# The first head pair's k and v as float32 over two hardware queues, a new order for the opening, and four stores on another queue, in a fused attention and mixer kernel

## The chip, the cores and the metric

One core of a Trainium2 chip runs the kernel. The metric is device time in microseconds of one execution, as the median of a few runs. The core has a matrix engine (PE, with its weight loads as PEld), a vector engine (DVE), a scalar engine (ACT), a general engine (POOL, GpSimd) and a sync engine (SP). Work moves between memory and SBUF on 16 DMA engines; SP and ACT issue transfers over hardware queues, POOL over a software queue, which is the only one of the three on which this kernel converts float32 to bfloat16 on the way.

## What is computed

Linear attention with projected keys and values, and then a token and channel mixer, on batch 8, 8 heads, 1024 tokens and head size 64. All inputs and the output are float32.

```python
def _attn_ref(q, k, v, E, F):
    k_proj = np.einsum('ks,bhsd->bhkd', E, k)
    v_proj = np.einsum('ks,bhsd->bhkd', F, v)
    scale = 1.0 / np.sqrt(q.shape[-1])
    scores = scale * np.matmul(q, k_proj.transpose(0, 1, 3, 2))
    scores = scores - np.max(scores, axis=-1, keepdims=True)
    attn = np.exp(scores)
    attn = attn / (np.sum(attn, axis=-1, keepdims=True) + 1e-09)
    return np.matmul(attn, v_proj)

def _moe_ref(x, w_tok1, w_tok2, w_ch1, w_ch2):
    xt = x.transpose(0, 2, 1)
    h = np.maximum(xt @ w_tok1, 0.0) @ w_tok2
    u = x + h.transpose(0, 2, 1)
    h2 = np.maximum(u @ w_ch1, 0.0) @ w_ch2
    return u + h2
```

E and F are 64x1024, w_tok1 1024x256, w_tok2 256x1024, w_ch1 512x1536, w_ch2 1536x512.

## The kernel before

**Stages.** One batch is attention ("front"), then the token mixer (token1, token2), then the channel mixer in two blocks of 512 tokens (up and down; block j belongs to batch j // 2, so there are 16). The channel mixer uses seven products for each 2x2 block product, and so sums of weights are made once by DVE (`combine`, L476: "W1" from w_ch1, three sets of four sums; "W2" from w_ch2, two sets of four). While batch b's up and down products run on PE, the front of batch b + 1 is threaded between them.

**The opening.** Batch 0 has nothing to be threaded into. Its heads go in pairs: pair (2, 3) first, then (4, 5), (0, 1), (6, 7). For a pair, PE turns q (L618), projects k and v with E and F (L521, sixteen matmuls), turns the projected k (L574), forms the scores (L637), ACT takes the exponential (L652), PE multiplies by the projected v (L672, `attend`), and DVE divides (L686, L692). E and F arrive as float32 in `o_t[0]`, a buffer that later holds outputs; PE turns them with a float32 identity (L462), and ACT and DVE copy a half each to bfloat16 (L465). Then come token1 (L1060) and token2 (L1092), the transposes of u (L1121), and the up products (L1180). Blank matmuls on zeros (L436) stand in PE's order where it waits: `FILLS` lists the places of the order ahead of which one is issued.

**Loads.** `LOADS` and the lists behind it issue k, v, q of batch 0 (256 KB in bfloat16 for two heads, 0.524 MB of float32 read), w_tok1 in two halves, w_tok2, six pieces of w_ch1 and four of w_ch2 on POOL's queue (L358), each with a conversion to bfloat16. E goes over SP's queue and F over ACT's. The code has a switch `HWK`, here 0, for sending the pair's k and v over those queues too.

**The order.** `Planner.add` numbers every piece of work (a job) as it is described. `ORDER` is a string of two base-64 digits a job and gives the order in which all 2203 jobs are issued; each engine executes its own in that order. `SPOTS` gives each accumulation a bank of PSUM. `LOADS`, the due times and the planner's durations have no other effect on the code that is issued than through the job numbers; `plan` checks that the order respects the dependencies. Read out, the loads on POOL come in this order:

```
k23 (identities) q23 v23 q45 k45 v45 k01 v01 q01 k67 q67 v67
w_tok1 (two halves)  w_tok2  w_ch1 (six pieces)  w_ch2 (two)
batch 1: k, v of heads 0 to 3   w_ch2 (two)   batch 1: the other loads
```

and PE's first jobs are a blank in float32, two in bfloat16, a second in float32, the transposes of E and F, q23, seven blanks, the projection of k23 and v23.

**Stores.** A down block stores two halves (L1326); all go over POOL's queue but those of the last block (`finish`), which name SP and ACT.

**Normalisation.** `rdn_t` holds the reciprocals of the attention's sums, in two tiles for even and odd pairs.

Of the kernel before, what the change touches and what calls it, by code (L numbers as in the profile page):

```python
# [15 lines left out]
    "0R030T0Q050P0S0408060U070W0V001L0X011M02091E0A1F1G1I1H1J0B1K1N1j1O0C1P1k1c0D1Z1d1Q1e1g1f1h1i0E1R1S1l"  # L16
    "1T1m1W1X0s1U0H0u0w0t0v1n0z0G0x0+1+0F0y0-201-101a1Y24111b1V26250J1812271B19151A1621130I14281C1D1u291o"
    "172S230K2A2T221p1r1q2N2O1v1s2B1t2E1x2P0M2C2U1w2Q1y2V2F1z2R2X2K2W2D2Y2H2G2Z2a2L2I2c2J2b2d2M2l0L2x2m2h"
    "2y2e3B2f2n2i2g2p2o2z3C2q2t2+2-2u2j2r0O302k332v2s0Y37342w310N3L0Z0a353M3d3I3H3D3v323J3N36383R3O0c3E3P"
    "3e0d4c0e3Q3j3K0g3h0f393F3i0b3S3A3f3T3k0h3g3U3-3l3V3G0i3w3X9w3n3W3Y3z4d3m3x3+4u4Y3y4a3p4v4Z403q4g410k"  # L20
    "4w3o5A424x4y0l5B4e0j4h5p4b4f454j464i4k3r5C4z0m43475D5E4l444-0o4m503s4o4n3t4+4p5q525t514B5F4q5r4C495s"
    "530p544D3Z5y3u5w0q5H3bA15x4J3c3a6B5u5I554K5z4r4G4L5K5v4A4H9v5L9x6D484I5+6E0r6F564M6C5-6G6O4N6A606P6Q"
    "626H6I6L4O636561646Z6J674s666K4EA26a57684F6M6b696N4Q0n6f4P6U6g6R6W4R6S6h6Y4U4S6V6c6i6T6X5S4T6d6j6k6u"
    "6l6e5T6m6n6x6+6v5U6o4V6-6y6z716p5a6q4W5G705b725J746r7A73756s765M6t776wA35N7B5O585Q787C5R4t5X5P795Y7J"
    "7F7K7D7G7H7Q7EA57I5Z7L7R5dA759A85eA65VA95fAAA45W5c5h5g5i7V7S5l7TAD7Z7X4X5m5j7a7n5k5n7b7o7W7d5o9z7M7e"
    "7p9-7c7O7q7g7P7r7h7N7f7sAF7i7uAH7Y7lAG7t7m7v7jAJ837wAIANAK7x84ALAOAhAM7z7yAiAP877kAj857U7+88AQAb8986"
    "ARAS8AAcAdAk8BAWAlAm8L9yAZ8CAYAeAT8DAfAaAg8FAUAXAV8M8G8EENB3At7-Az8N8mAEA+8+8i8n8TA-EO8k8oAuAvABAn8H"
    "8U8pB4B5AC8-8q81B0Aq8r92Ao8J90Ap938QArAs8jB6AwB18tB2B795Ax8uB88R8l91Ay8s96B9948v8w9G978x8yBB9H988SBD"
    "999I8KBE9KBCBF8z8WBGEP8VEQ9L9ABABI9N9BBJBH9O9+8X9JBKBNA0BLBO8Y9QBM829MBPBRBSBV8I8aBWBQBTBk9R80BYBXBl"
    "8bBZBUBn9PBc8OBdBa9SBeBfBpBbBh8PBgBmBiER9CBj8ZBo9YEVES9TBr9ZEUBqET8eBs9aEW8f8c9UBu8d9g9W9E9hEYBtC1Bz"  # L30
    "9dEZC2B-9iBwC59VC3BxC69eC48gC89D8hEbC9Bv9bEdC0Ec9c9FEfEj9fCBEeEgEkElCC9jB+EmEhEi9kEn9XEpEr9lC7EoCFCA"
    "By9nCGEsEtCDEq9oCEEu9mCJCHEvEwExCI9r9pCKCXEyEz9qCLCYCME+CNCZEaE-F09sCaILCOCPF19tIMCbDACREXCcF2F4F3Cd"
    "CQ9uF5CeF6CpCfF7FBDCChCSFCDEF9CqDFFADSCiCgFDCrDICTFEDGDJF8FGCjFHFFDHFLDTFICxCkFMFJFPClDUCmFKDLDBDVFQ"
    "FNDDDMFTCVCyINFUFRFODKCnFWDWFXCuDXDNFYCvCzFaCwFVDZFbDQDaC+DRFiFcDODcFSDPFZFdFfFeIPFjFgDdCUFhFlIRDYIT"
    "DkDbISCsIQCWDlFkIUIOC-CoFmFnDeD0CtFoFpDoFqD2DpD1D3FxIXDmD4D6DnIWFzFsFrDrD5FtDqDsFuF-DtD7G0DfDuD8G1Dv"
    "DwF+G2DgG3E0FvG4E1DiDxFwIZE2DyG6IbD+E8G7DjE9IcDzIdGDEAIaE5FyGEG9DhIeGAE6IfD-IhIgGHIiGFIjGIG5GGIkG8IY"
    "GVInE7GKMKIoGBImEBGCGLIsIlECItIuIpGNIqIrIvGOE3IwEDGWE4IxI-GZJ0EEIyGaEFJ1EGIzI+EJEHGXJ5EIJ2GYGcJ3J4GJ"
    "MJGdHQJ7IVJ9J8GbJAD9H8GfGeJBHCGMJCGhJ6JEH9GPJFGiJDGgJJHAHDJGEKHRGQJHJKGRHGJIGTHEHHMLJLMMJNHSJMHUGSHT"
    "HJHVJOGnJPELHFJRHKGjJTEMHXHBJSGlGoJUGpHIJVHMHLJWHNGsGUHYJYHiJQJZHaJXGtHbHOHjJbHPGvJaHmHWJcHnJgJdGwJe"
    "MNGuJfGxGmHZGyMPGkJhHpHcMOJjMRHkMSMQJkGzHlHdHoHqHeJnGqHrJlJoHsGrMVG+HtHuG-JiJzJmH0J+HvH4JpH1JvJsH2H+"  # L40
    "JtJqH3H-HwJxJ-I0JwH5JrK0K1JyJuHyMXK2HxI6MYHgMaK4HzH6I7MZK5HfKBI3I8KCK7MbHhMcK8KDMdQIMeMfKEKFMgMTMhI4"
    "KGK3I5MiK6KIMmI9KJIAMjMkKLIBMnKMK9MoMpKTMlKHKAKUMqI1MrMsQKIDL7MtKXMuMvKZKYIEKKMwL6KVIFKaL8I2IGMxKbMy"
    "KNKWH7ICKdMzKcKeLgM+LAM-IHLBKON0IIN1N3LEN2KfLFKlKgLON5KmLPIJN7KhIKLCN6N8LHMWN4N9LILSL9QHNAKPLQLDNCMU"
    "KiLRNBNDLKLTNENHKRKnLGKjNFLJLVNGKSKqNILLNJLhLMNKLWKrLNNPNLKtNMNQNNKkLiNOKsNSLkNTLYKuKQLZNWLjQJNUNXKw"
    "LlNVKoKvKpNZNRKxNYLUNaNeNbLnNcQLLXNfNdKyKzLaQMNhQOLbNjLmLoNiK+QNLpQPNgQQK-LcLqL0NlLrL2LeL1LsNmLyLtQT"
    "LzLuNnNoL+L3NtLwNxNkM4NyL4NqO9LxL5M5NvOANwNzNuOBM6N+M1NpOCODNrN-OEM2O0NsQVM3O2QWLvO1LdO3M7QXO4O5QYOG"
    "O7OHM8O8QZOFO6M9QaL-OIQdLfOJOLQeQbOKQfMBOMM0QcMCMAQgMDQlQkMFQmMEQnQhORQjP4QUMGP6QiONQRP8OSQoP7P9OXQS"
    "QpQqOVUGPAMHOWQuUFOTPBQvQwOYOUMIQrPCOZQsQtOjPDOaQxQ+PFQyQzObQ-OdR0OcPMOePGOkPNP5PIR1R5PJR3PEOlOPPOPQ"
    "OfPPOrOhR6PHPROsR4R7R2PTR8PSPURAR9RBOoRCPVOpOgUIRFOQRDRGOqPWREPKOtPXPeRJRHOiPfRKRNRLPYRIROOuPLRQPZUH"
    "PiRRPgRcOOPhRSOvRMRTRPRUOwUJRdRVPjRWPaRXUNRfUKRZRYOyULRaRhUMPlRgRbReUOPmPwRiPkRjPnPxRkOzPcPoOmO+PpRl"  # L50
    "RmPyO-PqRnOnRrRoQ2RtOxRvPrQ3RwRpP0Q4RqP1RxP2S7RyPsRzPuUPPbR+P-UQRuPvURS0RsQ0S8S1UUSBUVQ1S9SCS3UWSAQ5"
    "PdUTUXS4SEUYUZUSR-SDSFS2UaSGQ6UbUdS5Q7SJUePtUfUcQ9UgUhSPT3SHSKSQUoQASIUpS6STT2UrUqSUSRT6UsSSQBSWUlUt"
    "QCSXPzUmT7T4P+UnUiQ8TASZUjUkShSLT8UxUuT9QDUvSaUwSVUzQESYU-SiU+V0TBSbT5QFV1TCSNV2QGTDSjUyV4P3TETcScV5"
    "V3TFSpV6SqSdSOV9SfV7VASeTGTdVDSMTKV8THTeSrTIVHTJVBVISmVETLVFVCSnVKTgVLVMThTMSoVJTfVOVGTjTNVPVWTkTOVQ"
    "TiTPVRTlVTSsVNStVUVXTRVSTmTSSgVZVVTQTnVaTuTTToSuSkTpTWTqSwTXSxTYVdVYSySlTsSzTvVeTUSvVbVlTVVgVpVnS+Vf"
    "VqVcS-TwVmVtT0U0VuVoT1W1VhU1W2TaViVwVjVrVxU2W5VkWJW6VvWKTzVyT+WNT-V-W8W0VzU3WOW9W7VsU4WAV+WQTrWPTZWR"
    "WLWSW3WDU5W4X0TtWBWyWTTbWCXIWMWzWVW+WUTxWEX1TyWFU7U6U8WWX4W-U9UBWXWbUAWZX2XaX3UCX5WcXbUDXJX7WYXcWdWH"
    "X6XdWGXMX8WgXNX9WhXPXCXQXAXDXeWiWjXfWaXOXBXEXKXGWmXRXLWIWkXUWlWnXVXhWoWeXiXWXgWqXjWrXmWfXnXkXoXSWsXs"
    "XTWpWtXtXlXHUEXYWuXZXuXpWvXqXFX-XXX+WwXxWxXyXvY9XzXrY0XwY1Y4Y2Y3Y6Y5Y7YAYDY8YBYCYJYFYEYMYGYKYNYHYLYO"
    "YIYPYQ"  # L60
)
SPOTS = (
    "3024101126436327273643040127120236363170420436171063240217145624732113405063774765765024721257605205"
    "6726211311072323401724223063354705252601467407364317023117417326261333177136413604752570156153207422"
# [4 lines left out]
FILLS = (21, 21, 21, 21, 21, 21, 21, 27, 27, 30, 36, 36, 36, 36, 49, 62, 62, 66, 66, 79, 79)  # L69
# [20 lines left out]
HWK = 0  # L90
# [97 lines left out]
def kernel(  # L188
# [13 lines left out]
    nc = tc.nc  # L202
# [40 lines left out]
    def tile_of(shape, dtype, name):  # L243
        return sb.tile(shape, dtype, tag=name, name=name)
# [15 lines left out]
    for i, queue in enumerate((nc.sync, nc.scalar)[:HWK]):  # L260
        queue.dma_start(out=kv32[i], in_=(k, v)[i][0, 0:2].rearrange("h (p si) d -> p h si d", p=P))
# [33 lines left out]
    rdn_t = [tile_of([P, NJ, 2, 2], F32, f"rdn{i}") for i in range(2)]  # L295
# [82 lines left out]
    lead = (1.95, 2.45, 3.2)[HWK]  # L378
    for i in range(HWK):
        pl.add("SPQ", 1.6 + 1.1 * HWK, 1.6 + 1.1 * HWK, lambda: None, writes=[("kv32", i)], prio=-1001)  # L380
        if i:
            act(
                1024, lambda: nc.scalar.copy(out=v_sb[:, 0:2], in_=kv32[1]),
                reads=[("kv32", i)], writes=[("v", 0), ("v", 1)], prio=-100,
            )
        else:
            dve(
                1024, lambda: nc.vector.tensor_copy(out=k_sb[:, 0:2], in_=kv32[0]),
                reads=[("kv32", i)], writes=[("k", 0), ("k", 1)], prio=-100,
            )  # L390
# [55 lines left out]
    opening = [warm(zero), warm(zero), warm32(), warm32()]  # L446
# [1115 lines left out]
```

## Time and profile before

| What | us |
|---|---|
| median of three runs | 415.72 (415.28 to 415.97) |
| the profiled execution, its own time | 415.69 |
| its span, first to last instruction | 413.9 |
| PE busy | 406.4 (98%) |
| DVE busy | 355.9 (86%) |
| ACT busy | 221.9 (54%) |
| POOL busy | 66.8 (16%) |

The span is what the profile covers; the 1.8 us between it and the execution's time lie around it. Times of single instructions are counted from the span's start. The granted clock of PE is 0.999 over the whole execution.

The opening's landmarks, from the timeline and from the DMA issues with their time to landing (issue plus time to landing):

| What | us |
|---|---|
| E and F issued; landed | 0.74 and 0.76; 3.9 and 4.6 |
| k23, q23, v23 landed | 6.5, 7.9, 10.0 |
| first projection (k23, v23) begins | 9.91 |
| q45, k45, v45 landed | 11.3, 12.6, 13.8 |
| k01, v01, q01 landed | 15.1, 16.4, 17.7 |
| k67, q67, v67 landed | 19.0, 21.4, 22.3 |
| w_tok1 halves, w_tok2 landed | 23.6, 24.8; 27.3 |
| first token2 group begins | 28.15 |
| first up product begins | 33.95 |
| w_ch2, first two pieces landed | 37.6, 39.4 |
| batch 1, k and v of heads 0 to 3 landed | 42.0, 44.6 |
| w_ch2, last two pieces landed | 46.5, 48.4 |
| first down product begins | 52.1 |
| last instruction of DVE ends | 410.94 |

Here k23 stands for k of heads 2 and 3, and so on. In a row of windows the columns are the stretch, its length and, for each engine, busy time and the number of instructions that start in it, then PE's granted clock, the DMA share and the GB/s; bytes are counted as written, so a converting load counts half of what it reads. The share is a sum over queues and can pass 1.

### The profile page before, as it was taken

The page shows a single profiled execution, that of the slowest core. Times are in us where ns is not written, and L with a number is a line of the kernel's source. Part 1 is how long each engine was busy: PE and PEld are TensorE (multiplying, and loading weights), DVE is VectorE, ACT ScalarE, POOL GpSimd, SP SyncE. Part 2 cuts the span into 40 slices and gives each one's busy share as a digit, 9 for nine tenths or more (in the row PEclk, how much of TensorE's full clock was granted, in tenths as well). Part 3 has the DMA queues.
Part 4 walks back from the last instruction along what each step waited for, and adds up shares of the span by engine and source line. Part 5 has one row for each costly group of instructions (what it writes and reads, how often), then busy time and mean ns, then how long its engine had stood idle before and what let it go on. Part 6 is the DMA issues. An engine that isn't in the chain of part 4 may idle for free.

```text
span 413.9 us, 9589 instructions
## 1 busy us (share of the span) xinstructions
PE 406.4 (98%) x3909; PEld 344.4 (83%) x3911; DVE 355.9 (86%) x773; ACT 221.9 (54%) x429; POOL 66.8 (16%) x105
## 2 busy tenths in 40 slices
PE   8899999999999999999999999999999999999996
PEld 4489888688888888979988899888988798998896
DVE  2289899779999999989979798898989899988686
ACT  1647884258635664574754646455644745445520
POOL 8544021021102120112001112012100001010010
PEclk9999999999999999999999999999999999999999
DMA  8999999997998897978966869873996212251115
GB/s 153 205 202 204 207 190 192 160 172 170 189 166 168 201 170 143 166 156 156 245 118 127 133 148 178 143 167 89 180 227 118 52 51 103 52 115 39 52 69 187
DMA packets 93755, 61.69 MB, mean 149 GB/s; under 512 B 59024, under 2 KB 89232, under 8 KB 93712
## 3 DMA queue, kind: packets, MB, share of 16 engines
q0 software_dynamic: 35088, 45.09, 55.7%
q1 hardware_dynamic: 58256, 15.47, 22.8%
q8 instruction: 30, 0.49, 0.5%
q10 hardware_dynamic: 368, 0.52, 0.3%
q14 instruction: 13, 0.11, 0.1%
HBM read 59.24 MB, written 16.78 MB: 184 GB/s over the span
## 4 chain that ended last, share of the span: by engine, by line
PE 92%; DMA 4%; DVE 2%; POOL 1%; issue 1%; POOLq 0%; DVEq 0%
PE psum L1289 36%; PE psum L1180 35%; PE psum L991 5%; PE psum L875 4%; PE psum L672 3%; PE psum L521 3%; DMA q_sb<-in_q_dram 3%; PE psum L637 2%; DMA v_sb<-in_v_dram 1%; PE psum L712 1%; PE psum L1060 1%; PE psum L736 1%; DVE u L1105 1%; PE psum L1092 1%; PE psum L618 1%
## 5 line engine op out<-in xcount | busy, mean ns | idle before, releaser
L1289 PEld LDWEIGHTS <-G 128*128 128x128 bf16 x1356 | 130.0, 98 | 18.3 <-issue 3.5
L1289 PE MATMUL psum<-wc_sb,G 128*128 128x256 bf16 (+1 forms) x780 | 101.5, 271 | 0.0
L1180 PEld LDWEIGHTS <-wc_sb 128*128 128x128 bf16 x768 | 73.9, 98 | 10.5 <-issue 2.1
L1202 ACT ACTIVATE G<-psum 128x512 bf16<-128x512 f32 x96 | 56.2, 601 | 44.8 <-PE psum L1180 44.3
L1289 PE MATMUL psum<-wT,G 128*128 128x256 bf16 x576 | 75.6, 273 | 0.1
L1216 DVE TENSOR_TENSOR G<-G 128x512 bf16<-128x512 bf16 (+1 forms) x140 | 69.4, 515 | 0.8
L1180 PEld LDWEIGHTS <-wT 128*128 128x128 bf16 x576 | 55.3, 98 | 7.3 <-issue 0.6
L1180 PE MATMUL psum<-S,wc_sb 128*128 128x256 bf16 x384 | 56.2, 273 | 0.0
L1180 PE MATMUL psum<-S,wT 128*128 128x256 bf16 x384 | 56.0, 273 | 0.1
L1180 PE MATMUL psum<-uT,wc_sb 128*128 128x256 bf16 x384 | 55.5, 273 | 0.0
L1326 POOL DMA_DIRECT2D out_dram<-o x30 | 16.4, 548 | 212.7 <-DVE o L1332 171.2
L692 DVE TENSOR_TENSOR x_sb<-psum,rdn 128x256 bf16<-128x256 f32 (+1 forms) x88 | 46.7, 540 | 1.8
L1332 DVE TENSOR_TENSOR o<-psum,u 128x512 f32<-128x512 f32 x59 | 39.9, 681 | 3.7 <-PE psum L1289 3.3
L1208 ACT COPY ub<-psum 128x512 f32<-128x512 f32 x48 | 28.1, 588 | 23.4 <-PE psum L1180 18.5
L652 ACT ACTIVATE a<-psum 128x512 bf16<-128x512 f32 x64 | 34.9, 603 | 8.5 <-PE psum L637 8.3
L1161 DVE CUSTOM_DVE_ANT_0 G<-psum,ub 128x512 bf16<-128x512 f32 x48 | 32.7, 683 | 6.9 <-PE psum L1180 6.6
L1223 ACT COPY psum<-psum 128x512 f32<-128x512 f32 x48 | 27.6, 579 | 18.6 <-PE psum L1180 13.0
L1161 DVE CUSTOM_DVE_ANT_0 G<-psum,ua 128x512 bf16<-128x512 f32 x48 | 32.6, 684 | 5.3 <-PE psum L1180 4.4
L1208 ACT COPY ua<-psum 128x512 f32<-128x512 f32 x48 | 28.3, 590 | 14.0 <-PE psum L1180 13.6
L1180 PE MATMUL psum<-uT,wT 128*128 128x256 bf16 x192 | 28.7, 273 | 0.0
L358 POOL DMA_DIRECT2D v_sb<-in_v_dram x18 | 13.3, 742 | 75.4 <-PE psum L1180 22.7
L672 PE MATMUL psum<-vb,a 128*128 128x130 bf16 x256 | 25.3, 220 | 0.0
(102 smaller groups left out, 499.4 us busy)
## 6 DMA issues: line engine op xcount, KB each, us to landing
out_dram<-o POOLq DMA_DIRECT2D x30, 512.0 KB, 3.8
k_sb<-in_k_dram POOLq DMA_DIRECT2D x14, 512.0 KB, 11.2
v_sb<-in_v_dram POOLq DMA_DIRECT2D x14, 512.0 KB, 7.3
q_sb<-in_q_dram POOLq DMA_DIRECT2D x14, 512.0 KB, 9.2
wc_sb<-in_moe_w_ch_dram POOLq DMA_DIRECT2D x6, 256.0 KB, 11.9
wc_sb<-in_moe_w_ch_dram POOLq DMA_DIRECT2D x4, 384.0 KB, 13.3
k_sb<-in_k_dram POOLq DMA_DIRECT2D x4, 256.0 KB, 7.9
q_sb<-in_q_dram POOLq DMA_DIRECT2D x4, 256.0 KB, 8.1
```

Source lines behind the costliest of these rows:

```text
L652: lambda g=g, half=half, bk=bk: nc.scalar.activation(out=a_t[g][:, half], in_=bank(bk), func=ACT.Exp, scale=scale),
L672: nc.tensor.matmul(view()[:, k, c].rearrange("p i d -> p (i d)"), a_t[g][:, c, at : at + P], vb[:, g].rearrange("k i d -> k (i d)"), start ...
L692: lambda: nc.vector.tensor_tensor(out=x_sb[:, rows, g * P : (g + 1) * P].rearrange("p (n c) (i d) -> p n c i d", c=2, i=2), in0=view()[:, ...
L991: nc.tensor.matmul(view(X_OF[n])[:, r, :], tok2_of(n, i, r), T[n] if n in T else h[B[n]], start=(n in (1, 7) and r == 0), stop=True, skip_ ...
L1161: nc.vector._custom_dve(TENSOR_ADD_SAT, out=out, in0=in0, in1=in1, s0=FMAX, s1=0.0)
L1180: nc.tensor.matmul(t[:, c, :], w1_of(n, dd, 2 * m + c), a_of(j, n, dd), start=(n in (1, 7) and c == 0 and dd == 0), stop=(c == 1 and dd == 1),
L1202: lambda: nc.scalar.activation(out=G[:, n, cs], in_=view(src), func=ACT.Relu),
L1208: 512, lambda: nc.scalar.copy(out=dst, in_=view("y")), writes=[(name, s % 2)],
L1216: 512 * len(both), lambda: f(out=G[:, n, c], in0=G[:, a, c], in1=G[:, b, c]), ps=False,
L1223: 512, lambda: nc.scalar.copy(out=view("y"), in_=view("x")), takes=[bk["y"]],
L1289: nc.tensor.matmul(to, G[:, G_OF[n], cc, t * P : (t + 1) * P], w2_of(n, cc)[:, cut], start=(n in opens and (t == 0 or alone) and cc == 0), ...
L1332: 512, lambda: nc.vector.tensor_add(out=dst, in0=view(src), in1=u_of(sh, dh)),
```

## The change

Four edits.

1. k and v of heads 2 and 3 are no longer converted on the way. They are read as float32 into `o_t[1]` and `o_t[2]`, head 2 over SP's queue behind E and head 3 over ACT's behind F (256 KB each, four loads). Four new copies convert them: DVE takes k2 and v2, ACT k3 and v3. The two loads leave POOL's list.
2. The order, the banks and the blanks are new. POOL's loads now come as: k45 (identities) q23 v45 q45 q01 v01 k01 q67 k67 v67, w_tok1, w_tok2, w_ch1 (six), batch 1's k and v of heads 0 to 3, w_ch2 (four), the rest of batch 1. PE's first jobs are one blank in bfloat16, one in float32, one in bfloat16, four blanks, the transposes of E and F, twelve blanks, the projection of k23 and v23, the transposes of q23, and the projection of k45 and v45. There are 26 blanks from `FILLS` for 21, and one float32 blank less. Behind the opening the order differs in small ways, until on each engine it is the same as before: for PE from the first up products of block 4 on.
3. `rdn_t` becomes one tile with eight places, taken in turn.
4. The stores of blocks 13 and 14 (two each) go over SP's queue.

```diff
-FILLS = (21, 21, 21, 21, 21, 21, 21, 27, 27, 30, 36, 36, 36, 36, 49, 62, 62, 66, 66, 79, 79)
+FILLS = (11, 11, 11, 11, 26, 26, 26, 26, 26, 26, 26, 26, 26, 26, 26, 26, 36, 36, 36, 36, 40, 61, 61, 73, 73, 86)
...
-    ("k", 0, 2), ("v", 0, 2), ("q", 0, 2), ("k", 2, 2), ("v", 2, 2), ("q", 2, 2),
+    ("k", 0, 2), ("v", 0, 2), ("q", 0, 2), ("q", 2, 2),
...
-    for i, queue in enumerate((nc.sync, nc.scalar)[:HWK]):
-        queue.dma_start(out=kv32[i], in_=(k, v)[i][0, 0:2].rearrange("h (p si) d -> p h si d", p=P))
+    for i, src in enumerate((k, v)):
+        for h, queue in enumerate((nc.sync, nc.scalar)):
+            queue.dma_start(out=kv32[i][:, h], in_=src[0, 2 + h].rearrange("(p si) d -> p si d", p=P))
...
-    rdn_t = [tile_of([P, NJ, 2, 2], F32, f"rdn{i}") for i in range(2)]
+    rdn_t = tile_of([P, 2 * HP, NJ, 2, 2], F32, "rdn")
...
+    pl.add("SPQ", 4.5, 4.5, lambda: None, writes=["EF"], prio=-1003)
+    for i, (name, to) in enumerate((("k", k_sb), ("v", v_sb))):
+        pl.add("SPQ", 7.8 + 1.6 * i, 7.8 + 1.6 * i, lambda: None, writes=[("kv32", i)], prio=-1002 + i)
+        for h in range(2):
+            (act if h else dve)(
+                512,
+                lambda i=i, h=h, to=to: (nc.scalar.copy if h else nc.vector.tensor_copy)(
+                    out=to[:, 2 + h], in_=kv32[i][:, h]
+                ),
+                reads=[("kv32", i)], writes=[(name, 2 + h)], prio=-100 + i,
             )
...
-    opening = [warm(zero), warm(zero), warm32(), warm32()]
+    opening = [warm(zero), warm(zero), warm32()]
...
+    attended = iter(range(2 * B * HP))
+
     def attend(g, half, due, span):
+        at = next(attended) // 2 % (2 * HP)
+
...
-            rdn = rdn_t[g % 2][:, 2 * half + jn[0] : 2 * half + jn[0] + n]
+            rdn = rdn_t[:, at, 2 * half + jn[0] : 2 * half + jn[0] + n]
...
-            queue = queue or nc.gpsimd
+            queue = queue or (nc.sync if NSB - 3 <= j else nc.gpsimd)
```

The new strings for `ORDER` and `SPOTS` are left out.

More of the change, by code (lines that the diff above doesn't have):

```diff
@@ L21 @@
[L21 to L30, printed above, removed]
@@ L56 @@
[L56 to L60, printed above, removed]
+    "0U0001040B0W0X0A0V0C0D0a090Y08070F03020E0Z0b0G06050H1I1P0I1J1g1Q1h0J1K1M1N1O1i0M1R1l1n1S1m1L1k1T110K"
@@ L377 @@
     w2t = moe_w_tok2.rearrange("(tc p) s -> p tc s", p=P)
[L378 to L389, printed above, removed]
+    lead = 0.0
+    pl.add("SPQ", 4.5, 4.5, lambda: None, writes=["EF"], prio=-1003)
[8 more added lines that the diff above has]
+                reads=[("kv32", i)], writes=[(name, 2 + h)], prio=-100 + i,
             )
@@ L452, in identities @@
         make_identity(nc, ident32)
-    opening.append(pl.add("POOL", 1.0, 3.2, identities, writes=["ident"], prio=-150))
+    opening.append(pl.add("POOL", 1.0, 1.4, identities, writes=["ident"], prio=-150))
     pl.opening = opening
@@ L670, in mm @@
                     for c in range(2):
-                        at = (2 * half + jj) * P
+                        s0 = (2 * half + jj) * P
                         nc.tensor.matmul(
-                            view()[:, k, c].rearrange("p i d -> p (i d)"), a_t[g][:, c, at : at + P],
+                            view()[:, k, c].rearrange("p i d -> p (i d)"), a_t[g][:, c, s0 : s0 + P],
                             vb[:, g].rearrange("k i d -> k (i d)"), start=True, stop=True,
                         )
-            keys = [("rdn", g % 2, 2 * half + jj) for jj in jn]
+            keys = [("rdn", at, 2 * half + jj) for jj in jn]
             xs = [("x", 2 * g + i, half) for i in range(2)]
```

81 lines of the change are left out of this document (47 added, 34 removed).

## The prediction

> **What bounds the kernel now.** I read four views in this order: the page's 40 slices, the chain that ended last, the opening in one-microsecond windows, and the DMA queues of the first 45 us. Times are microseconds from the span's start.
>
> ```profile
> PE   8899999999999999999999999999999999999996
> DVE  2289899779999999989979798898989899988686
> DMA  8999999997998897978966869873996212251115
> ...
> PE 92%; DMA 4%; DVE 2%; POOL 1%; issue 1%; POOLq 0%; DVEq 0%
> ```
>
> The first two slices (20.7 us) are the only ones ahead of the last in which PE is under nine tenths, and DMA is nearly full there. From the third slice on PE is the bound, so the end moves one for one with the time at which PE becomes dense. The chain's 4% of DMA lies in the opening:
>
> ```profile
> 1.31 0.79 POOL k_sb L358
> 3.20 0.67 POOL q_sb L358
> 3.87 6.17 DMA v_sb<-in_v_dram
> 10.34 11.12 DMA q_sb<-in_q_dram
> ...
> 38.73 7.51 PE psum L1180 x68
> ```
>
> The chain of waits rests on the third software-queue load (v of heads 2 and 3, landed at 10.0) and the eleventh (q of heads 6 and 7, 21.5). Compute that lies between two landings costs nothing. The windows show whether the DMA engines are full:
>
> ```profile
> 2.00:3.00 1.00, 1.00 (x2) 0.15 (x1) 0.00 (x0) 0.63 (x1) 0.86 (x5) 1.00 0.78 213
> 3.00:4.00 1.00, 1.00 (x4) 0.63 (x3) 0.00 (x0) 0.00 (x0) 1.00 (x3) 1.00 0.86 311
> 4.00:5.00 1.00, 1.00 (x3) 0.42 (x2) 0.00 (x0) 0.00 (x0) 1.00 (x2) 1.00 0.99 141
> ...
> 8.00:9.00 1.00, 1.00 (x12) 0.65 (x11) 0.41 (x1) 0.00 (x0) 1.00 (x3) 1.00 0.76 122
> ...
> 12.00:13.00 1.00, 1.00 (x14) 0.65 (x15) 0.00 (x0) 0.59 (x2) 0.44 (x2) 1.00 1.25 207
> ...
> 25.00:26.00 1.00, 1.00 (x19) 1.00 (x19) 0.93 (x5) 0.00 (x0) 0.74 (x1) 1.00 1.18 188
> ```
>
> The last two columns are the DMA share and the GB/s. The share runs at 1.24 when the engines are full (from 11 on). From 2 to 11 the shares of the nine windows fall short of 1.24 by 0.46, 0.38, 0.25, -0.01, 0.10, 0.14, 0.48, 0.13 and 0.02, together 1.95, or 1.95/1.24 = 1.6 us of lost DMA time. Of it 0.9 us lies before 5: POOL issues one load (1.28 to 2.11), makes the identities (to 3.20) and only then issues the second. From 25 on PE starts 19 to 22 matmuls per us, mostly of 128 columns; the timeline has twenty of these in 1.28 us, so PE is dense, and behind that only small stalls are left to win.
>
> **The queues: two loads out, four in.** Two casting loads of 0.524 MB (float32 read) leave POOL's queue; the same 1.05 MB comes as float32 over SP and ACT, in pieces behind E and F. Its price comes from E and F, the only such loads in the trace:
>
> ```profile
> q0 software_dynamic: 9318, 8.07, 112.8%
> q1 hardware_dynamic: 80, 0.26, 2.0%
> q10 hardware_dynamic: 80, 0.26, 1.4%
> ```
>
> Shares are of 45 us. E and F (0.52 MB) took 3.4%, 1.53 us of all engines; 1.05 MB is then 3.06. The casts took 112.8%, 50.8 us for 16.1 MB read, so a load is 1.65 and the two that go are 3.30. In clock time, at 1.24, that is +2.5 and -2.7. **The bytes cost the same by either road**; what can be won is the holes, since the new pieces are issued at about 1.3 to 2.45 (0.57 each behind E at 0.74 and F at 0.76), when the engines have little else. Two values: only the holes before 5 fill (0.9), or all up to 11 (1.6). A check on the latter: full from 2.0, the engines do E, F and k, v (4.6), three software loads (4.95), and 1.5 that was in flight before too (the shares of 2 to 10 sum to 8.0 and 6.5 had landed), together 11.0/1.24 = 8.9, so the third software load lands at 10.9. The loads after it come every 1.27 (before: 10.0 to 19.0 for seven), so the tenth and now last of the attention lands at 19.8; before, the twelfth landed at 22.3, behind a jump of 2.5 after k of heads 6 and 7, which I can't explain. If a jump of 0.8 above the spacing returns, it is 20.6. The gain is 1.7 to 2.5 that way. I take **-1.6**, the holes counted directly, and keep 0.9 and 2.5.
>
> [...]
>
> **Casts.** Four new copies of 128x512 from float32, two on DVE, two on ACT. No row shows one from SBUF; the nearest are 0.69 (DVE) and 0.59 (ACT) from PSUM, L465, and 0.42 for bf16 in SBUF, L476. The last stands between v's landing and the first projection. If the hardware pieces go first, v lands at 2.0 + 4.6/1.24 = 5.7; if POOL's queue gets an equal third, at 2.0 + 6.9/1.24 = 7.6, both plus a tail of about 1. With 0.7 it is ready by 9.3. In PE's order stand 12 blank matmuls ahead of that projection: they cover it (seven took 1.67, so 12 take 2.9; the E and F transposes end near 7.1, so 10.0). Before, the projection began at 9.91. Price 0; without the cover, up to the late part, and then the projection of heads 4 and 5 is next. ACT's first cast stands ahead of the copy of E and F; DVE's likewise: both halves must be out before 10.0, with about 1 us to spare. The two more hardware issues on ACT (1.1 us) push its table load to about 2.5 to 3.8; ACT is idle from 2.6 to 6.66.
>
> **The new order of the opening.** q of heads 6 and 7 goes from eleventh to eighth, k to ninth, v to tenth. Before, q landed at 21.5 and its chain (transposes, the copy of 1.01, scores, two exponentials of 1.08 together) ended at 24.75, 2.45 behind v's landing. Now k is the head of the chain: projection 0.63, copy 0.58, transpose 0.23, copy 0.27, scores 0.41, exponentials 1.08, about 3.2 behind k and 1.9 behind v: **-0.55**. PE is then dense at about 25.0 - 2.15 = 22.85 with the same work done. The next gate is wt2: landed 27.25 before, 25.65 now, and the first token2 group (28.15 before) would stand at 26.0, so it is not held. One float32 blank less and 26 blanks for 21 lie in time in which PE waits: 0.
>
> **Behind the opening.** From PE's order, the first product of the first down block comes 20.5 us of matmuls behind the first token2 group, 23.6 before (0.109 for one of 256 columns: the chain has six in 0.66). Batch 1's k and v (2.6 each) now go ahead of all four loads of w_ch2. So the load it needs last (39.4 before for the second of the four, now the third) lands at 39.4 + 5.2 + 1.9 - 1.6 = 44.9; PE is there at 26.0 + 20.5 = 46.5. DVE meets the first sum of w_ch2 at about 42.9, and its second load lands at 43.0. That is tight: DVE is full there (0.97 to 1.00 a window). I take **+0.2** and keep -0.5 (fewer small stalls; PE waited 0.34 at 37.89 for such a sum before) and +1.2. One more reciprocal tile per pair removes orders, no instruction: 0.
>
> **The four stores.** Blocks 13 and 14 now issue on SP: 0.57 each for 0.55 on POOL. Ahead of them on SP there is no transpose left, and behind them only the last block's own stores, the first at 408.05; the last of the four is ready at 404.1. The end hangs on DVE at 410.94 and its store. Price 0, with 0.3 either way; if the cover of 3.4 us were gone, an issue of 0.57.
>
> **Sum.** -1.6 - 0.55 + 0.2 = -1.95: span 413.9 to 411.95. The profiled execution took 415.69, the median of three is 415.72; so 413.8.
>
> **The rivals.**
> *Shared engines*: packets of the new pieces hold up POOL's queue, and the holes from 6 on stay, for instance because they came from the engines' uneven load. The gain is then 0.9 at most, and the order's gain shrinks, because ACT's chain of about 10 us of copies and exponentials behind the second projection becomes the limit: 415.72 - 0.9 + 0.2 = 415.0. For it: 0.76 at 8 to 9 with five loads issued. Against: the first holes are plainly missing issues.
> *Written bytes (slower)*: a float32 load writes twice what a cast does, and if the SBUF side were the limit, 1.05 MB would cost 1.05/0.204 = 5.1 us. At 2.7 saved and 1.6 filled, the software stream is 0.8 later; k and v land near 2.0 + 1.2 + 5.1 = 8.3 at best and some 2 later beside POOL's queue, the blanks no longer cover the first projection, and the order's 0.55 is lost behind it: 415.72 + 0.8 + 0.2 = 416.7. It decides from a price of 4.3 on. Against it: 311 GB/s at 3 to 4, above the 204 of full casting.
> *The w_ch2 order*: the opening gains 2.15, but the four late loads stall DVE at 42.9 by over 1 us, then PE: 415.72 - 2.15 + 1.2 = 414.8.
>
> **Chances.** Forecast 0.54; shared engines 0.18; written bytes, or anything else slower, 0.14; w_ch2 order 0.14. A measurement of this kernel can tell about 0.2%, 0.83 us, from no change. Faster than 414.9 gets 0.5 from the forecast, half of the w_ch2 case and a third of the shared: 0.64. Slower than 416.55: 0.14 and a little: 0.16. The rest, 0.2, is no change. The range runs from all bounds at their good end less what can't all come together (-3.1, 412.6) to the shared case with the w_ch2 stall, 416.2; the forecast's own is 412.6 to 414.9.
>
> **What would show it.** Right: DMA share near 1.24 from 2 or 3 on; the third software load landed by 11 and the tenth by 20.6; the first projection within 0.4 of 10; PE at 19 matmuls per us from about 23; the first token2 group at about 26. Wrong: v's float32 landing after 9.5; the q1 and q10 shares over twice those of E and F per byte; a DVE or PE wait of over 1 us for wc_sb between 40 and 50; a last product that keeps its distance to the first token2 group only with longer gaps.

## The result, and the profile after

The changed kernel took 416.15 us (median of 22 runs, 415.76 to 417.83), the kernel before 415.57 on the same chip (22 runs, 414.80 to 416.33): a ratio of 1.0018, 95% interval 1.0010 to 1.0026. Two later controls on other chips gave 1.0026 (1.0013 to 1.0039) and 1.0022 (1.0012 to 1.0031). 413.8 was forecast, a gain of 1.95; the kernel became 0.6 slower. The time lies in the stated range, but only by its far end, 416.2, which stood for the shared case with a stall for w_ch2, and that stall did not come. Three of the 22 runs took 417.6 to 417.8 at a mean granted clock of 0.994 to 0.996; the other 19 lie between 415.76 and 416.52 (where that comes from is told with e12).

The profiled execution has a span of 414.4 us (413.9 before). Its page, with the slices and the chain that ended last:

```profile
PE   7899999999999999999999999999999999999996
DVE  2399899879999999989979798898988899988686
DMA  8999999497999898979956869882998212251124
...
PE 91%; DMA 5%; ACT 2%; DVE 1%; issue 1%; DVEq 0%; ACTq 0%; POOLq 0%
```

PE's first slice fell from 8 to 7 and everything behind it is as full as before. The chain of waits now names two loads in the opening, the first on POOL's queue (k of heads 4 and 5) and k of heads 6 and 7:

```profile
1.28 7.21 DMA k_sb<-in_k_dram
8.77 11.46 DMA k_sb<-in_k_dram
```

The opening in windows (columns as in the prediction; DMA share and GB/s last):

```profile
2.00:3.00 1.00, 1.00 (x2) 0.15 (x1) 0.00 (x0) 0.56 (x1) 0.85 (x5) 1.00 0.89 193
3.00:4.00 1.00, 1.00 (x4) 0.37 (x3) 0.00 (x0) 0.73 (x1) 1.00 (x3) 1.00 1.00 387
4.00:5.00 1.00, 1.00 (x7) 0.56 (x6) 0.00 (x0) 0.00 (x0) 1.00 (x2) 1.00 0.99 265
...
7.00:8.00 1.00, 1.00 (x7) 0.39 (x4) 0.00 (x0) 0.00 (x0) 1.00 (x2) 1.00 1.11 331
8.00:9.00 1.00, 0.54 (x3) 0.11 (x1) 0.85 (x2) 0.23 (x1) 0.41 (x2) 1.00 1.18 263
9.00:10.00 1.00, 0.00 (x0) 0.00 (x0) 0.46 (x2) 0.39 (x1) 0.49 (x1) 1.00 1.23 205
12.00:13.00 1.00, 1.00 (x18) 0.55 (x13) 0.71 (x3) 0.26 (x1) 0.56 (x1) 1.00 1.25 206
...
25.00:26.00 1.00, 1.00 (x20) 1.00 (x20) 1.00 (x5) 0.00 (x0) 0.32 (x1) 1.00 1.42 197
```

The share doesn't reach 1.24 until 9 us: with float32 pieces on two hardware queues it stands at 0.99 to 1.11 from 3 to 8, though 265 to 387 GB/s are written there and 204 in full casting. And PE stands still from 8.9 to 10.2, which it didn't do before. The timeline of PE says for what (start, busy time, then in brackets the idle time and its releaser):

```profile
6.64 1.67 PE L435 MATMUL psum<-zero 128*128 128x512 bf16 x7
8.63 0.22 PE L520 MATMUL psum<-k_sb,EFT_sb 128*64 128x128 bf16 x1 [0.31 <-DVE k_sb L385]
10.20 0.24 PE L520 MATMUL psum<-v_sb,EFT_sb 128*64 128x128 bf16 x1 [1.35 <-DVE v_sb L385]
```

The blank matmuls end at 8.3, and the projection waits 1.35 us for the cast of v2, whose float32 piece landed at 9.70. The queues over the first 45 us:

```profile
q0 software_dynamic: 8919, 7.69, 106.9%
q10 hardware_dynamic: 368, 0.79, 5.7%
q1 hardware_dynamic: 368, 0.79, 5.0%
```

**One yardstick for all that follows.** I count the matmuls that belong to the computation by their columns (the same in every kernel here; blanks left out), on a scale on which all of them come to 387.6 us, and read the time at which the same amount of them has been started; the scale is my own and not a measured time. A count from the shapes in the traces, with matmuls that start in pairs at half, gives 384.6 in place of 387.6 and leads within some 0.2 us of these. (In the changed kernel's first projection a pair of k and v starts every 0.057 us, from 10.28 to 10.62; the transposes of q behind it, eight full matmuls of as many columns, start every 0.057 too.) The table gives that time against the first profile of before; a minus is a lead. e9, e16 and e15 are the controls told below. e5, a third profile of the changed kernel, is left out: it ran a stretch at half clock (0.50 from 12 to 14 us, told with e12) and is 0.7 to 0.8 behind after 12 us of work.

| useful matmul work done, us | before, time | changed | before, 2nd (e9) | before, 3rd (e16) | changed, again (e15) | mean changed less mean before |
|---|---|---|---|---|---|---|
| 2 | 7.98 | +2.42 | +0.11 | -0.49 | +1.68 | +2.18 |
| 12 | 28.09 | -0.46 | -0.32 | -0.32 | -0.74 | -0.39 |
| 50 | 67.44 | -0.30 | -0.21 | -0.33 | -0.70 | -0.32 |
| 90 | 108.52 | -0.26 | -0.43 | -0.32 | -0.34 | -0.05 |
| 120 | 139.47 | +0.18 | -0.42 | -0.31 | +0.11 | +0.39 |
| 290 | 312.23 | +0.22 | -0.42 | -0.28 | +0.14 | +0.41 |
| 387 (end) | 409.89 | +0.55 | -0.42 | -0.28 | +0.37 | +0.69 |

So the opening gained 0.4, not 2.15, and the rest gave back 1.1: 0.3 up to 108 us, 0.4 between 108 and 139, and 0.3 in one event near 320. The tail is untouched: from the end of the last matmul to the end of the span it is 3.30 us before and 3.28 now.

### The profile page after: what moved, and what is told of

The parts are those of the page before. It is cut to its first block, busy times and chain, and to the rows that moved or that the text cites. A ratio compares the mean times of both kernels' runs of the same rounds, so it can differ in the third digit from the quotient of the medians.

```text
span 414.4 us, 9611 instructions
## 1 busy us (share of the span) xinstructions
PE 406.4 (98%) x3914; PEld 344.0 (83%) x3914; DVE 357.4 (86%) x775; ACT 222.5 (54%) x431; POOL 63.2 (15%) x99
## 4 chain that ended last, share of the span: by engine, by line
PE 91%; DMA 5%; ACT 2%; DVE 1%; issue 1%; DVEq 0%; ACTq 0%; POOLq 0%
PE psum L1292 36%; PE psum L1183 34%; PE psum L878 5%; DMA k_sb<-in_k_dram 5%; PE psum L994 4%; PE psum L675 3%; PE psum L520 3%; PE psum L636 2%; PE psum L1095 1%; PE psum L1063 1%; PE psum L739 1%; PE psum L715 1%; ACT ub L1211 1%; PE psum L617 0%; PE psum L1124 0%
## 5 line engine op out<-in xcount | busy, mean ns | idle before, releaser
L1329 POOL DMA_DIRECT2D out_dram<-o x26 | 14.3, 550 | 181.0 <-DVE o L1335 125.0
```

## The experiments

Ratios and times are against the kernel before in runs on the same chip. No kernel leaves anything out of the computation.

**Controls: e5 and e15 are the changed kernel, e9 and e16 the kernel before, unedited.**

> The changed kernel itself once more, as the control for the three kernels beside it. Theory (the change loses 0.2 to 1.2 us whatever the chip): ratio 1.0005 to 1.003, lead over before 0.0 to 0.5 us once 12 us of matmul work are done, given back by 0.4 to 0.8 us until 131 us of work. The step of 0.3 us near 320 us of the span (a sum that waits for a transfer of transposed u) is single in theory: it is gone or stands elsewhere here. Rival (the new orders cost this chip more than the first one): ratio above 1.004.

> The changed kernel, as control on this chip. All theories: 416.0 to 416.4 us in most runs, one run in six or seven 1.2 to 1.6 us longer with the mean clock at 0.994 to 0.996, ratio to before 1.0015 to 1.003.

> The kernel before itself, profiled once more. In e7, whose opening is that of before instruction for instruction, the third load landed at 8.98 us and the weights of token2 at 26.65, against 10.04 and 27.25 in the profile that the prediction was made from, and the DMA shares from 4 to 8 us were 1.22 to 1.30 against 0.99 to 1.25. Theory (the holes in the load stream that the 1.6 us were read from belong to that one execution, not to the kernel): third load under 9.5 us, token2's weights under 26.9, 0.4 to 0.8 us ahead of the first profile at 12 us of work, span 413.0 to 413.5. Rival (the first profile is typical and e7's stream was early by chance): third load at 9.8 to 10.2, span 413.8 to 414.2.

> The kernel before, a third profile. Theory (the start of its load stream differs from execution to execution): third load anywhere from 8.9 to 10.1 us, and the time at 12 us of matmul work moves with it, within 0.2 us. Rival (only the first profile was late): third load at 9.5 to 9.7 as in e9.

e5 took 416.29 (before 415.18), e15 416.05 (before 415.23): the ratios are as the theory said. Two parts of e5's theory failed: its profile was behind at 12 us of work, not ahead (half clock, see e12), and the event near 320 us, called single, came again in both. e9 took 415.20 (ratio 0.9994, 0.9985 to 1.0002), e16 415.42 in its one run. The third load landed at 10.04 in the first profile, 9.61 in e9 and 9.12 in e16, between the theory and its rival for e9, and with the theory for e16. But the time at 12 us of work did not move with it: e16's third load came 0.92 earlier and its lead is 0.32. What it moved with is the last load of the attention (v of heads 6 and 7), which landed at 22.26, 21.91 and 21.83. Here are the windows of e16, to be held against those in the prediction:

```profile
2.00:3.00 1.00, 1.00 (x3) 0.15 (x2) 0.00 (x0) 0.63 (x1) 0.85 (x5) 1.00 0.51 160
3.00:4.00 1.00, 1.00 (x4) 0.63 (x3) 0.00 (x0) 0.00 (x0) 1.00 (x3) 1.00 1.01 375
4.00:5.00 1.00, 1.00 (x3) 0.42 (x2) 0.00 (x0) 0.00 (x0) 1.00 (x2) 1.00 1.18 193
8.00:9.00 1.00, 1.00 (x6) 0.48 (x5) 0.69 (x1) 0.00 (x0) 1.00 (x3) 1.00 1.06 118
```

Same instructions, other holes: 0.99 became 1.18 from 4 to 5, 0.76 became 1.06 from 8 to 9. Summed from 2 to 11 as in the prediction and divided by 1.24, the holes are 1.57 us in the first profile of before, 1.06 in e9 and 1.31 in e16; in the changed kernel they are 1.07, in e5 1.06 and in e15 1.39. The mean of three is 1.31 before and 1.17 after. **Measured so, the float32 loads filled 0.1 us of holes**, less than the 0.5 by which three profiles of one kernel differ. Whether a share of 1.0 to 1.1 is all that the engines do with such a mix of loads, or leaves room, no run here shows. The first group of token2, as PE's weight loads show it (min/median/max ns, then the first and last start), before (first profile and e16) and changed (first and e15):

```profile
L1092 PEld LDWEIGHTS <-wt_sb x64: 142/146/161, 28.2 to 33.6; 128*128 128x128 bf16 x64
```

```profile
L1092 PEld LDWEIGHTS <-wt_sb x64: 142/146/155, 27.8 to 33.3; 128*128 128x128 bf16 x64
```

```profile
L1095 PEld LDWEIGHTS <-wt_sb x64: 142/146/157, 27.6 to 34.0; 128*128 128x128 bf16 x64
```

```profile
L1095 PEld LDWEIGHTS <-wt_sb x64: 143/147/158, 27.5 to 33.9; 128*128 128x128 bf16 x64
```

Against e16 the changed kernel starts this group 0.2 to 0.3 earlier, against the first profile 0.6 to 0.7; the forecast had 2.15.

**e3 and e4, e8: the two halves of the change by themselves.** e3 has the new order with converting loads, e4 and e8 the old order with the float32 loads. All three keep the changed stores and the one tile of reciprocals.

```diff
 # e3, against the changed kernel
-    for i, src in enumerate((k, v)):
-        for h, queue in enumerate((nc.sync, nc.scalar)):
-            queue.dma_start(out=kv32[i][:, h], in_=src[0, 2 + h].rearrange("(p si) d -> p si d", p=P))
...
-    ("k", 0, 2), ("v", 0, 2), ("q", 0, 2), ("q", 2, 2),
+    ("k", 0, 2), ("v", 0, 2), ("q", 0, 2), ("k", 2, 2), ("v", 2, 2), ("q", 2, 2),
```

> The changed kernel without the float32 loads and the four copies: k and v of heads 2 and 3 are converting loads on POOL again (k23, identities, q23, v23, k45, v45, q45 and on as in the changed order); the order of PE, DVE and ACT is the new one. Theory (the float32 loads bring the load stream forward by 0.7 to 1.1 us, and that is the whole gain of the opening): 0.5 to 1.0 above the changed kernel, 416.6 to 417.1. Rival (the float32 loads bring nothing, because they hold up POOL's queue by as much as they save): 416.1 or less.

> The old order with the float32 loads of k and v of heads 2 and 3 over SP and ACT and their four copies; POOL's loads in the old order without those two (q23, identities, q45, k45, v45 and on); one float32 blank is replaced by four in bfloat16. Theory: the later loads land 0.7 to 1.1 earlier and the old order behind uses it, 414.6 to 415.1. Rival (v over SP's queue lands near 9.7 and its copy and the projection come 0.9 later than before, and the opening's chain carries that on): 415.6 or above.

> Before's order with the changed kernel's float32 loads, as e4, but the cast of v2 stands ahead of the copy of the transposed q, the seven blank matmuls ahead of the first projection are gone, and 12 blank matmuls stand ahead of the transposes of q instead. Theory (e4 lost 2.0 us to its blanks and to the cast queued behind the copy, and the old order loses nothing later): first projection's matmuls from 9.8 to 10.3 us in place of 12.66 less its own time, lag to before between -0.8 and +0.2 us from 12 us of work to the end; time 1.6 to 2.4 us under e4 by the lag, that is 0.8 under to 0.4 us over before. Rival (the float32 loads leave the later first-batch transfers no earlier and the casts load DVE and ACT): the lag comes back to +1 us or more by 20 us of work.

e3 took 418.23 (ratio 1.0075, 1.0051 to 1.0098), e4 418.03 (1.0065, 1.0044 to 1.0086), e8 417.42 (1.0049, 1.0031 to 1.0068). At 12 us of work they stand at +0.43, +2.00 and +1.34, at the end at +1.67, +1.85 and +1.52. **In these profiles each half alone loses 1.5 to 2 us where both together lose 0.6.** (e4's holds 1.70 us of missing clock, shown in the last section; its two runs at a mean clock of 0.998 and 0.999 took 416.4, 1.4 over before.) e3 lies above what its theory and its rival named; e4 and e8 came out at the rival's number, but not for its reason. The new order needs k and v of the first pair early; the old order wants q of heads 2 and 3 while those come in and leaves PE with nothing to do (2.76 us in e4, until that q has landed). e8's mending was half a success: the cast got ahead of the copy, but its 12 blanks took 4.18 us (2.75 in the changed kernel), and the first projection began at 11.99 where 9.8 to 10.3 was expected. e4 and e8 lose nothing between 108 and 139 us (e8 0.35 near 320, e4 nothing).

**e1: the four stores back on GpSimd's queue.**

```diff
-            queue = queue or (nc.sync if NSB - 3 <= j else nc.gpsimd)
+            queue = queue or nc.gpsimd
```

> The changed kernel with the four stores of blocks 13 and 14 back on POOL's queue. Theory (the loss lies in the opening's small gain and in the order behind it): nothing changes, 416.1, within 0.1 of the changed kernel. Rival (the stores on SP's queue cost the difference): 415.6, the time of before.

e1 took 417.15 (1.0052, 1.0033 to 1.0071), where the theory had 416.1 and the rival 415.6. PE starts its last matmul 0.3 later than in the changed kernel, a difference that stands in the opening already (-0.04 against -0.46 at 12 us of work), and the tail is 4.12 in place of 3.28, since the last stores land 2.6 and 2.8 us after their issue in place of 2.0 and 2.2. That tail isn't the stores' queue alone: e3, with the stores on SyncE's, has 4.17; e2, e4, e6 and e8 have 3.69 to 3.73; e7 and e14, with the stores on GpSimd's, 4.29 and 3.34. What makes it stays open, and e1 to e8 are compared by the table's yardstick, not by their times.

**Which stretch loses: e2, e6, e7, then e13, e14 and e17.** Each takes one order to some place and the other behind it. The lines below tell the edit in short form; in the kernels it is the strings `ORDER` and `SPOTS` that differ.

```diff
 # e2, e6, e13, e17: P = 175, 174, 400, 439
-order = changed
+order = changed[:P] + [job for job in before if job not in changed[:P]]
 # e7, e14: P = 174, 396
-order = before
+order = before[:P] + [job for job in changed if job not in before[:P]]
```

e6 and e7 also bring the weight loads into the order of the second part; e2 doesn't.

> The changed kernel up to the first up product; behind that the old order (and the old banks but for one). Theory (the opening is 0.45 us ahead per piece of PE work, and the new order behind it loses 0.64 by 131 us): the 0.45 stays, so 415.1, with PE's lead over before at 0.4 or more from 40 to 400 us. Rival (the lead is lost to the loads: batch 1's k and v now land ahead of all of w_ch2, whatever the order behind): 415.7 or more.

> The changed kernel's loads, casts and opening up to the last token2 products of batch 0 (place 174), and behind it the order of before, with the weight loads in the order of before too. Theory (the new order behind the opening gives back 0.6 us, the old one nothing): the lead of 0.0 to 0.5 us at 12 us of work stays to the end; time 0.5 to 0.8 us under the control, 0.0 to 0.4 under before. Rival (the loss belongs to the opening's loads, which run into the later stages through the load stream): the lead is lost by 131 us of work here too, and the time is within 0.2 us of the control.

> Before's loads and opening up to place 174, and behind it the changed kernel's order with its order of weight loads; stores on GpSimd's queue as before. Theory (the new order behind the opening gives back 0.6 us by itself): level with before until 45 us of work, then 0.5 to 0.8 us behind from 131 us on; time 0.5 to 0.8 us over before. Rival (the new order behind is harmless or better and the loss follows from the opening): time within 0.3 us of before, or under it.

e2 took 420.16 (1.0110, 1.0085 to 1.0136): at its seam DVE's first sum of w_ch2 needs loads that the other order issues last, and PE loses 3.9 us between 24 and 50 us of work. That is the price of the "w_ch2 order" case when the orders don't match. e6 took 416.64 (1.0041, 1.0026 to 1.0057) and e7 417.84 (1.0063, 1.0047 to 1.0080), 0.35 over the control where the theory had it 0.5 to 0.8 under, and 2.7 over before where 0.5 to 0.8 was expected. Their seams cost 0.6 and 1.2 by 50 us of work, so they answer the question only behind it: from 90 to 120 us of work e6 loses 0.13, e7 0.43, as the changed kernel does. The clean test needed a place at which both orders have done the same (at 400 they differ in one job):

> The changed kernel to place 400 of its order (both orders have issued the same jobs there), and behind it the order of before. Theory (the changed order's losses of 0.35 us near 110 us and 0.1 to 0.2 near 130 us of the span come from its places behind 400): no PE gaps at 109.2, 109.9, 129.4 and 130.1, the lead of 0.3 us over before's first profile stays to 290 us of work, the event near 320 us may stay; time 0.4 to 0.7 us under the control. Rival (the losses come from what the opening leaves behind, not from the order): gaps of the same size between 100 and 135 us, time within 0.2 us of the control.

> Before to place 396, and behind it the changed kernel's order, stores on GpSimd's queue. Theory: level with before to 88 us of work, 0.4 to 0.6 us behind from 131 us on, time 0.4 to 0.6 us over before, more by up to 0.9 us if the last stores land 2.6 to 3.0 us after their issue as in e1 and e7 and not 2.0 as in before. Rival: within 0.2 us of before.

e13 took 415.71 (ratio to before 1.0020, 1.0009 to 1.0032; the control e15 416.05), e14 416.86 (1.0040, 1.0028 to 1.0052; 1.6 over before, where 0.4 to 0.6 and up to 0.9 for the stores were expected: its seam, priced at nothing, cost 1.2). All waits of PE's weight loads from 105 to 135 us (total, times, longest), in the control e15:

```profile
PEld L1292 <- issue: 0.4, 1, 0.4
PEld L1292 <- DVE G L1219: 0.4, 1, 0.4
PEld L1183 <- DVE S L810: 0.2, 1, 0.2
PEld L878 <- issue: 0.2, 1, 0.2
PEld L636 <- issue: 0.2, 1, 0.2
PEld L520 <- issue: 0.2, 1, 0.2
PEld L1183 <- issue: 0.2, 1, 0.2
```

and in e13:

```profile
PEld L1292 <- DVE G L1219: 0.5, 1, 0.5
PEld L1292 <- issue: 0.4, 1, 0.4
PEld L636 <- issue: 0.2, 1, 0.2
PEld L520 <- issue: 0.2, 1, 0.2
```

Three waits are gone: one for a sum of S, and two in which PE waited for nothing that the profile shows. e14 has all three again. From 90 to 120 us of work e15 and e14 lose 0.45 and 0.44, e13 0.01 (the seams cost 0.2 in e13 and 1.2 in e14, both ahead of 90). **So 0.4 us of the loss belongs to the new order behind the opening, and to nothing before it.** Two of the three pauses stand where the profile shows nothing to wait for, one of them inside a group of weight loads, so a sum of costs would not have found them:

```profile
109.24 0.10 PEld L878 LDWEIGHTS <-wt_sb 128*128 128x128 bf16 x1
109.55 0.31 PEld L878 LDWEIGHTS <-wt_sb 128*128 128x128 bf16 x3 [0.21 <-issue]
```

e17 moves e13's seam to a place that costs nothing.

> The changed kernel to place 439 of its order, the order of before behind. Theory (the opening leads by 0.2 to 0.4 us, the old order behind loses nothing but the event near 320 us): no gap at 71.2 us, lead over before's first profile 0.2 to 0.7 us until 290 us of work; time 0.1 to 0.3 us under e13, that is within 0.4 us of before on either side. Rival (any seam costs 0.2 us or more): as e13, 0.3 to 0.6 us over before.

e17 took 415.89 (1.0014, 0.9998 to 1.0030). Against its theory, which had the lead last to 290 us of work, it keeps 0.44 to 100 (0.32 at 120), then loses 0.35 in two pauses of the same kind near 194 and 196 us and 0.33 near 320, and ends at +0.36. Pauses that go at one place came back at another; three profiles with the old order behind a changed front (e6, e17, e18) have the pair near 194, a fourth (e13) doesn't. Before's own order shows none of them in three profiles. The event near 320 is a transfer of transposed u that took 5.8 to 6.0 us and not 4.2 to 4.4; in e3, whose loads convert, it is there too, and in e4, which has the float32 loads, it isn't. It stands in all eleven profiles with the changed opening, whatever the order behind, and in e8; it costs nothing in any profile with the opening of before (e7 and e14, which have the new order behind it, among them). So it goes with the opening and not with the order behind it; its cause wasn't found.

**e10 and e11: before, with loads ahead of the identities** (an attempt at the hole before 5 us without float32; in short form).

```diff
 # POOL's first jobs, e10 and e11
-load k2,3; identities; load q2,3; load v2,3
+load k2,3; load q2,3; identities; load v2,3
+load k2,3; load q2,3; load v2,3; identities
```

> Before, with one step moved: GpSimd issues the load of q2,3 ahead of building the identity matrices, 1.2 us earlier (about 1.99 in place of 3.14 us). Theory (the load stream is full from 4 us on when its start is not disturbed, and only what moves bytes ahead of 4 us brings it forward): the stream lands 0.2 to 0.5 us earlier than in e9's profile, time 0.1 to 0.4 us under before. Rival (transposes of E and F wait for the identities and the projection with them): no change within 0.2 us, or up to 0.4 us slower.

> As e10, with the load of v2,3 ahead of the identities as well. Theory: as e10 or 0.1 to 0.3 us better by the stream; the identities are ready near 4.6 us, with E and F at 3.9 to 4.5, so the transposes start 0.2 us later at most. Rival: the transposes of E and F become the last to arrive, first projection later by 0.3 us or more, time 0.2 to 0.6 us over e10.

e10 took 415.67 (1.0017, 1.0003 to 1.0032), e11 415.98 (1.0024, 1.0010 to 1.0039): the rival, for a reason that neither had. With q2,3 issued at 2.10 in place of 3.14 the first load landed at 7.57 in place of 6.0 to 6.5 and the second at 8.85 in place of 7.3 to 7.8, PE stood idle for 2.98 us waiting for it, and the share from 4 to 6 fell to 0.77 (1.12 in the first profile of before). In e10 the earlier issue didn't fill that hole but widened it; no row shows why.

**e12 and e18: the wait for v2 covered by blanks.** The trace of e5 shows what that wait can cost (busy time, granted clock, DMA share, GB/s):

```profile
8.00:10.00 2.00, 0.88 (x5) 1.00 1.21 236
10.00:12.00 2.00, 1.63 (x30) 0.93 1.24 204
12.00:14.00 2.00, 2.00 (x18) 0.50 1.24 205
14.00:16.00 2.00, 2.00 (x17) 0.72 1.23 203
```

Behind the idle stretch (1.17 us, to 10.05) the granted clock was 0.93, 0.50 and 0.72 in three windows of 2 us: 0.14 + 1.00 + 0.56 = 1.70 us of clock are missing, and by 14 us of the span this execution is 1.3 us behind the first one of the same kernel (+1.79 against +0.49 at 4 us of work).

```diff
-FILLS = (11, 11, 11, 11, 26, 26, 26, 26, 26, 26, 26, 26, 26, 26, 26, 26, 36, 36, 36, 36, 40, 61, 61, 73, 73, 86)
+FILLS = (11, 11, 11, 11, 26, 26, 26, 26, 26, 26, 26, 26, 26, 26, 26, 26, 26, 26, 26, 26, 26, 36, 36, 36, 36, 40, 61, 61, 73, 73, 86)
```

> The changed kernel with 17 blank matmuls in place of 12 ahead of the first projection, which cover the 1.35 us in which PE waits for v2. Theory (in 3 of 22 runs of the changed kernel, and in 2 of 11 of e5, the time was 1.2 to 1.6 us longer at a mean clock of 0.994 to 0.996; e5's profile has the clock at 0.50 from 12 to 14 us, behind the window in which PE was idle): no run is over 417 us, the other runs stay within 0.2 us of the changed kernel's 416.1 to 416.3. Rival (the slow clock has another cause): as many runs over 417 as before, about one in six.

> As e17 with the seam at place 446 and three more blank matmuls ahead of the first projection. Theory: no run with a mean clock under 0.997 (about one run in six of the kernels without the cover has one), the other runs within 0.3 us of e17. Rival (the blanks delay the projection, as e12's median of 416.53 against 416.05 to 416.3 may say): 0.2 to 0.5 us over e17.

e12 took 416.53 (416.29 to 416.89, nine runs), e18 416.20 (415.75 to 416.76, twelve); none of the 21 had a mean clock under 0.999. Without the cover it was 0.996 or less in 5 of 42 runs of the changed kernel and in 5 of 24 of e13 and e17. So the cover does what the theory said, though 0 of 21 against 10 of 66 alone would be a modest proof; the clock in e5's windows is the better one. But nothing is gained: with all runs counted the ratios are 1.0025 (1.0016 to 1.0035) for e12 and 1.0009 (0.9995 to 1.0022) for e18, against 1.0018 to 1.0026 and e17's 1.0014. e18's median lies 0.35 over that of e17's runs at full clock, the rival's part, but its seam differs too, and its profile shows no such delay; so the price of the cover isn't shown. No version tried was faster than the kernel before; e17 and e18 can't be told from it.

## Why the prediction was wrong, point by point

**The holes, -1.6: the step that failed.** "The holes counted directly" were counted in one execution. Counted in three of each kernel they shrink from 1.31 to 1.17 us, and the opening as a whole gained 0.4, not 2.15. The two values kept, 0.9 and 2.5, both assumed that a hole from a missing issue fills when something is issued. The float32 pieces filled the windows with a share of 1.0 to 1.1 and not 1.24, and in e10 a converting load issued earlier filled nothing either. What the stream did gain (v of heads 6 and 7 landed at 21.57, 21.27 and, in e5, 21.20, against 22.26, 21.91 and 21.83: 0.65 in the mean) is the lower price of the bytes (0.2 by the forecast's +2.5 and -2.7), 0.1 of holes, and 0.35 for which I have no row. The prices of the bytes were right: E, F and the four pieces took 10.7% of 45 us, 4.8 us, against 1.53 + 3.06 = 4.6.

**Landings.** The third software load was to land by 11 and did at 11.73, the tenth by 20.6 and did at 21.57; v's float32 landed at 9.70, over the 9.5 named as a refutation (8.91 in e15). That is nearer to the case in which three queues share equally (8.6 with its tail of 1, an estimate for which the forecast names no row; E and F, 1.53/1.24 = 1.2 us from 2.0 on, had landed 0.7 and 1.4 behind 3.2) than to the one in which the hardware pieces go first (6.7), and later than both. The first casting load took 5.2 us from issue to landing before and 7.2 now, beside the new pieces; how the engines divide their time among the queues, no run shows.

**Casts, 0.** Their length was right (0.43 on DVE, 0.62 on ACT). The cover was not: the blanks ended at 8.3 and not at 10.0, since the transposes of E and F ended at 5.7 and not at 7.1. In the first profile PE waited 1.66 us in all and the projection was through at 10.8; the stream hid that, but not the clock: 5 of 42 runs took 1.0 to 1.7 us more, 0.2 in the mean.

**The new order of the opening, -0.55.** Not seen. PE became dense at 24.0, not at 22.85, and the windows of ACT show why the earlier loads brought little (length, ACT's busy time and count, granted clock, DMA share, GB/s):

```profile
16.00:17.00 1.00, 1.00 (x2) 1.00 1.25 207
17.00:18.00 1.00, 1.00 (x2) 1.00 1.29 218
18.00:19.00 1.00, 0.96 (x4) 1.00 1.18 194
...
20.00:21.00 1.00, 0.98 (x3) 1.00 1.13 211
21.00:22.00 1.00, 1.00 (x3) 1.00 1.12 209
```

ACT is as good as full from 15 to 22 (0.90 to 1.00 a window, in the first profile of before 0.48 to 0.98 a window). In e15 and e5 the chain that ended last runs over ACT's copies and exponentials there; from e15 (start, time, what, with its end handed to DVE):

```profile
15.81 1.53 ACT qT L336 x2
...
20.01 1.09 ACT a L651 x2
...
21.52 0.25 DVE rdn L689 x2
```

So the prediction's "Compute that lies between two landings costs nothing" failed there: from 14.7 to 21.1 that chain names ACT and one transpose on PE and no landing, though k of heads 6 and 7 was there at 20.04. In the first profile the chain rests on that landing, at 20.23. The case "Shared engines" had this: a gain of 0.9 at most in the opening, the order's gain gone. e3, with the new order alone, is 0.64 behind the mean of before at 12 us of work, so the order by itself is no gain. The case was given 415.0, because it shared the next step with the forecast.

**Behind the opening, +0.2.** The loads of w_ch2 were fine: no wait for wc_sb of over 1 us, 0.1 lost from 12 to 50 us of work. The size of the rest was wrong: +1.1, just under the bound of +1.2, but for another reason than the one that the bound was made for. The small differences of order behind the opening were priced at nothing (with -0.5 kept for fewer small stalls); 0.4 of the 1.1 is theirs by e13 and e14, 0.3 is the event near 320, and 0.3 lies between 67 and 108 us, mostly in e15.

**The stores, 0 within 0.3**: right as far as the changed kernel goes, the tail is 3.3 in both. **Written bytes (slower)** gave 416.7, near the time by luck: its mechanism is one that the shares exclude (its price was 5.1 and decided from 4.3 on; for all float32 loads together 4.8 was measured, for the new ones alone 3.3). With the measured terms the sum is -0.4 + 1.1 = +0.7, against +0.6 to +1.1 in the medians.

## What to carry to other kernels

A gap read in the first ten microseconds of one trace is a sample (1.57, 1.06 and 1.31 us in three of the kernel before): profile the unchanged kernel two or three times and count the gap in each before it is priced as something to win, and ask by which row the engines ran full with the new kind of transfer. When a whole order is replaced, put the old order back behind the part that is meant to gain; places that differ only slightly can cost as much as the part gains (here 0.4 us each). If PE must wait in an opening, the wait can cost clock as well as its own length (1.70 us of clock behind 1.17 in e5), and a cover of blanks must be priced too: here it took the slow clock away and gained nothing.

## What the runs showed of the hardware

**Half clock behind a short idle stretch.** e5's profile loses 1.70 us of clock behind an idle stretch of 1.17 us, e4's the same sum (0.66 + 1.00 + 0.04) behind 2.76:

```profile
8.00:10.00 2.00, 0.79 (x8) 0.67 1.22 218
10.00:12.00 2.00, 2.00 (x8) 0.50 1.25 207
12.00:14.00 2.00, 1.86 (x22) 0.98 1.23 203
```

Six of e4's eight runs had a mean clock of 0.996 or less, four of twelve in e11 (idle 1.93 us), three of eleven in e10 (2.98 us, yet full clock in its profile). The kernel before, idle for 0.5 to 0.7 us in its three profiles, had it in 4 of 136. The first profile of the changed kernel idles for 1.35 us ahead of 10.20 and has a clock of 1.00 in every window from 8 to 15. So the length of the idle stretch alone doesn't decide it; what does, no run shows.

**Two loads issued together landed in no fixed order.** SP's and ACT's pieces of k were issued 0.04 us apart; they landed at 8.12 and 5.11 in the first profile, at 6.40 and 6.16 in e15, at 5.30 and 7.76 in e8.
